# Single scatters, expert weights on ScalarE's queue, and the next stage's loads inside a sort's end: a convolution with a routed expert layer

## The chip, the cores and the metric

The kernel runs on one core of a Trainium2 chip. The core has five engines that run beside each other, each working through its own list of instructions in order: TensorE (PE in the profile, with its weight loads as PEld), VectorE (DVE), ScalarE (ACT), GpSimd (POOL) and SyncE (SP), which here only starts DMA transfers. They meet through semaphores. All transfers run on 16 DMA engines; an instruction of SP, ACT or POOL starts one. The metric is device time of one launch in microseconds (us), lower is better; the time of a kernel is the median of its runs.

## The reference

Each of 8 sequences of 5696 tokens by 128 channels is convolved along the sequence with a filter of the same length (one filter per channel, written in the reference as a product of FFTs). Every token of the result then goes to one of 8 experts, the one with the largest gate logit:

```python
y = irfft(rfft(x, n=2*S) * rfft(h, n=2*S))[:, :S]      # per channel, x is [8, 5696, 128]
logits = y @ w_gate                                     # 45568 tokens, 8 experts
e = argmax(logits); g = softmax(logits)[e]
out = g * (relu(y @ w1[e]) @ w2[e])                     # w1 [8,128,1024], w2 [8,1024,128]
```

## The kernel before

**Stages.** The FFT length is split as 48 x 238, so that the transforms become matmuls with small constant matrices. The 8 sequences are worked in three groups of 2, 3 and 3. Each group passes three phases. Phase A (`steps_a`) transforms along one axis and stores U to DRAM. Phase B (`phase_b`) reads U back in blocks, multiplies by a 96 x 96 matrix for each of 120 frequencies (tile `xp`), by the filter's transform on DVE, adds on POOL (L524), and transforms back (tile `vp`), which ACT copies out for a store to V. Phase C (`phase_c`) reads V, does the last transform (tile `yp`), and finds each token's gate logits, its expert and its rank among the expert's tokens so far. POOL then writes every token's row (128 channels, gate value, token number) to its place in a DRAM table `SR` that is sorted by expert: an indirect DMA of 120 rows (`sort_one`, L608), 128 of them in a group. These are "the sort". When the last ranks of a stretch are known, `tables` works out on DVE which tiles of 256 rows are full and to which expert each belongs; for the very last stretch `fill` also writes dummy rows behind each expert's last token.

Phase A of the next group rides as a guest on phase C's steps (`Guest.begin`, `Guest.end`); what is left is done by `Guest.rest`.

**Experts.** The sorted tokens are taken in four parts of 37, 39, 28 and 81 tiles. Part 0 comes from the first group, parts 1 and 2 from the second, part 3 from the third. `pipeline` is a loop of steps, four to a tile: a tile's rows are loaded from `SR` (`load`, SP), turned on PE, split into two words on ACT and DVE, and each step does a quarter of layer 1 (L1055), the relu on ACT and its rest on DVE (`relu`, L1061, L1063), and a quarter of layer 2 of two steps before (L1075). After four steps ACT copies the result out (`drain`), PE turns it back, DVE multiplies by the gate (`emit`, L1093), and `deliver` scatters the two halves of 128 tokens to the output with two indirect DMAs on POOL (L1119). An expert's weights are four pieces of 512 KB (`load_w`, L1013 to L1028); a register tells whether the tile's expert differs from the one before, and if not the DMA is skipped. Parts 0 to 2 have one set of weight buffers, the last part two.

While a phase C of the second or third group runs, the POOL queue belongs to its sort. Finished expert tiles are then staged in DRAM (`leave`, the `STG` tensor) and brought back later (`recall`, tile `xb`), one in 6 steps; 48 tiles went this way.

**The order of the work.** Nothing is scheduled by the compiler; a small planner writes one fixed order for all engines (`run`). Streams are Python generators, each with a clock of its own that advances by the nanoseconds it yields (an expert step is `STEP = 1420`, an iteration of phase B 0.6 or 0.85 of it, a step of phase C 1.2 or 1.8 of it), and the stream whose clock is furthest behind emits next. After phase B of the first group three streams run: `rest` (phases C and B, group after group), the tail of the weight preparation, and `experts`. So an engine's list is this order filtered by engine, and an instruction that must wait holds everything behind it on its engine. `sort_one(after)` makes a sort scatter wait for a named ACT instruction, to spread the scatters over the stage; each ACT relu, each copy of phase C hands one out. In the first group's phase C the experts are off (`state["alone"]`), as no part is sorted yet. A part may be used once it is sorted, its table is there and (the last one) it is filled (`Part.ready`, `usable`).

Of the kernel before, what the change touches and what calls it, by code (L numbers as in the profile page):

```python
# [54 lines left out]
STAGED = 64  # L55
BACK = 6
HEAD = (0, 8, 8)
LEAD = (0, 6, 6)
# [11 lines left out]
def conv_moe(ctx: ExitStack, tc: tile.TileContext, I, out, B, S, D, E, F, split):  # L70
# [39 lines left out]
    class Part:  # L110
        def __init__(self, s, upto, tiles):
            self.s, self.upto, self.nt = s, upto, tiles
            self.sorted = self.tabled = self.filled = False
            self.lanes, self.fills = [], []

        @property
# [476 lines left out]
    state["base"] = base0  # L593
    state["alone"], state["prepped"], state["defer"] = True, False, False

# [8 lines left out]
    def sort_one(after=None):  # L604
        if not sorts:
            return
        pi, rt, b, pt = sorts.pop(0)
        s = nc.gpsimd.indirect_dma_start(  # L608
            out=SR[:, :],
            out_offset=IndirectOffsetOnAxis(ap=pi[:, b : b + 1], axis=0),  # L610
            in_=rt[:, b, :],
            in_offset=None,
            bounds_check=NROWS - 1,
            oob_is_err=False,
        ).ins
        tc.declare_no_dep(s, group="sr", reason="each row of the sorted tokens is written once, before it is read")
        tc.declare_no_dep(s, group="rows", reason="never a row that a tile has read")
        tc.add_to_no_dep_group("sr", s)
        if len(lanes) >= PIPE_LANES:
            tc.add_manual_dep(s, lanes[-PIPE_LANES].name, SYNC, reason="scatter lane")  # L620
        if after is not None:
            tc.add_manual_dep(s, after.name, SYNC, reason="scatters are spread over the stage")
        lanes.append(s)
        part_row()
        if pt is not None:
            pt.lanes = lanes[-PIPE_LANES:]
            pt.sorted = True

# [8 lines left out]

    def phase_c(gr, guest=None):
        g, nb, cb, cw, NI, ns = gr.g, gr.nb, gr.scb, gr.scw, gr.ni, gr.ns
# [96 lines left out]
        def logit_out(n, k):  # L736
            t = sb.tile([32 * cb, MP], F32, tag="lt", name=f"lt{g}_{n}_{k}", bufs=6)
            done = nc.scalar.copy(t, lbank.pop((n, k))[: 32 * cb, :MP])
            lts[n, k] = t
            sort_one(done.ins)  # L740
            if len(sorts) > ns:
                sort_one()
# [97 lines left out]
        for n in range(n_end + 1):  # L840
            for k in range(nsub):
# [15 lines left out]
                if guest:  # L857
                    guest.begin(1 if k == 0 and n >= sl else 2)
                yield cost if n < nu else cost / 2
# [9 lines left out]
                if k == 0:  # L869
# [6 lines left out]
                    if n - sl - 1 in closes:  # L876
                        pt = closes[n - sl - 1]
                        chores.append(tables(pt, state["base"]))
                        if pt is parts[-1]:
                            chores.append(fill(pt, state["base"]))  # L880
                chore(6)
                if at >= total_sub + LL:
                    break
        while sorts:
            left = len(sorts)
            chore(6)
            yield cost
            if len(sorts) == left:
                sort_one()
# [123 lines left out]
    def load_w(t, n):  # L1013
        pt, j = seq[t]
        z, fixed = home(t), j < sets(t)
        if n == 0:
            ew = nc.sync.value_load(pt.tab[0:1, 1, j : j + 1], min_val=0, max_val=(E - 1) * P)
            ch = None if fixed else nc.sync.value_load(pt.tab[0:1, 2, j : j + 1], min_val=0, max_val=1)
            regs[t] = (ew, ch)
# [5 lines left out]
        kw = {} if fixed else {"cond": ch, "cond_hint": False}  # L1025
        nc.sync.dma_start(dst, WD[n, ds(ew, P), :], **kw)  # L1026
        if n == 3:
# [62 lines left out]

    def emit(t):
        op, xr = obank.pop(t), rows.pop(t)
# [3 lines left out]
        if state["defer"] and slot[0] < STAGED:  # L1096
            leaving.append((STG[slot[0]], xr))
            slot[0] += 1
        else:
            pending.append(xr)  # L1100

    def leave():
        while leaving:
            dst, xr = leaving.pop(0)
            nc.sync.dma_start(dst, xr)
            staged.append(dst)

    def recall(count):
        if coming and coming[0][0] <= count - BACK // 2:
            pending.append(coming.pop(0)[1])  # L1110
        if staged and not coming and not state["defer"] and count % BACK == 0:
# [4 lines left out]
    def deliver():  # L1116
        xr = pending.pop(0)
        for s in range(2):
            sc = nc.gpsimd.indirect_dma_start(  # L1119
                out=out[:, :],  # L1120
                out_offset=IndirectOffsetOnAxis(ap=xr[:, s, D + 1 : D + 2].bitcast(I32), axis=0),
                in_=xr[:, s, :D],
                in_offset=None,
                bounds_check=B * S - 1,
                oob_is_err=False,
            ).ins
            tc.declare_no_dep(sc, group="out", reason="each token is written once")
            tc.add_to_no_dep_group("out", sc)
            if len(outs) >= PIPE_LANES:
                tc.add_manual_dep(sc, outs[-PIPE_LANES].name, SYNC, reason="scatter lane")  # L1130
            outs.append(sc)

    def usable(t):
        return seq[t][0].ready and state["prepped"] and not state["alone"]

    def pipeline(lo, hi):
# [3 lines left out]
        while True:  # L1140
            t, k = step
            while nrow < min(t + 4, hi) and usable(nrow):
                load(nrow)
                seen[nrow] = len(hist)
                nrow += 1
            while nw[0] < min(t + 3, hi) and usable(nw[0]):
                was, n = user[nw[0]], nw[1]
                if was is not None and was >= lo and passed.get((was, n // 2), -1) < 2 * (n % 2) + 1:
                    break
                load_w(nw[0], n)  # L1150
                nw = (nw[0], n + 1) if n < 3 else (nw[0] + 1, 0)
            act = step if t in xts and nw > (t, k // 2) else None
            hist.append(act)
# [5 lines left out]
            if act is None and old is None and to is None and ti is None:  # L1159
                leave()  # L1160
                recall(len(hist))
                if pending:
                    deliver()
                elif t >= hi and not (any(hist[-1 - LAG :]) or staged or coming):
                    return
                yield STEP if turned < nrow or any(hist[-1 - LAG :]) else None
                continue
            leave()
            recall(len(hist))
# [19 lines left out]
            if to is not None:  # L1189
                emit(to)  # L1190
            if pending:
# [9 lines left out]

    def rest():
        for gr in groups:
            if gr.g:
                yield from phase_b(gr)
            guest = Guest(groups[gr.g + 1]) if gr.g + 1 < len(groups) else None
            yield from phase_c(gr, guest)
            if guest:
                yield from guest.rest()

    DONE = object()

    def run(*streams, until=None, stop=()):
        live = [[0.0, i, s, share] for i, (s, share) in enumerate(streams)]
        held = []
        while any(t[2] not in stop for t in live):
            live.sort(key=lambda t: t[:2])
            it = live.pop(0)
            cost = next(it[2], DONE)
            if cost is None:  # L1220
# [107 lines left out]
```

## Time and profile before

| what | us |
|---|---|
| median of 3 runs | 2454.19 |
| lowest and highest of them | 2442.0, 2454.91 |
| the profiled execution, time | 2445.03 |
| the profiled execution, span from first to last instruction | 2443.3 |

The stages in the profiled execution, by the matmul lines that run in them (phase A L295, B L484, C L685, experts L1055):

| stage | from, to (us) |
|---|---|
| phase A of group 0, filter, then phase B of group 0 | 0, 275 |
| phase C of group 0 with phase A of group 1 | 290, 466 |
| end of the first sort, rest of phase A, first expert tiles | 466, 551 |
| phase B of group 1 with experts | 551, 828 |
| phase C of group 1 with phase A of group 2 and experts | 850, 1139 |
| end of the second sort, experts alone | 1139, 1192 |
| phase B of group 2 with experts | 1192, 1534 |
| phase C of group 2 with experts | 1550, 1830 |
| end of the third sort, experts alone | 1830, 1873 |
| experts of the last part, staged tiles brought back until about 2200 | 1873, 2443 |

How to read the profile's rows. A row of the table by stretches gives the stretch, its length, and for each engine its busy time with the count of instructions, then the clock granted to PE as a share of full speed, the share of time that the DMA engines were busy, and GB/s. A row of waits, "engine line <- releaser: total, times, longest", says how long an engine stood before instructions of that line and what ended it. In the order of time a row gives start, duration, engine, line, operation, the tiles written and read, and in brackets the idle time before with what ended it; SPq are the instructions of SP's own list. A row of one line's instructions gives the operation, its count, and shortest, median and longest duration in nanoseconds.

### The profile page before, as it was taken

What the parts mean: (1) busy time and instruction counts of PE and PEld (TensorE: products, weight loads), DVE (VectorE), ACT (ScalarE), POOL (GpSimd) and SP (SyncE); (2) the same over time, 40 slices, a digit from 0 to 9 for tenths busy, and PEclk for the clock granted to TensorE, in tenths of its full rate; (3) what the DMA queues carried; (4) which work ended last, traced back from release to release, by engine and by line L of the source; (5) the groups of instructions that cost most, each with busy time, mean ns of one, the idle gap of its engine ahead of it and who ended that gap; (6) DMA issues with size and microseconds to landing.
All of it is one profiled execution on the core that took longest, in us unless ns stands there. A gap on an engine that the chain in (4) does not pass through costs nothing. (4 is left out here: it accounts for less than half of the span.)

```text
span 2443.3 us, 46852 instructions
## 1 busy us (share of the span) xinstructions
PE 2144.8 (88%) x14070; PEld 1781.7 (73%) x14070; DVE 1582.2 (65%) x3937; ACT 1100.3 (45%) x2389; POOL 1196.8 (49%) x1289
## 2 busy tenths in 40 slices
PE   6899687469999899987899999988987899989997
PEld 4666344257677687777767677877877888889997
DVE  3599554439899677775698798566764444445554
ACT  4677443233333366653333343555643344434443
POOL 4466446715555326665246565166663444443332
PEclk8899899679999999998999999999998999999998
DMA  8999897469999778873788897666653443443330
GB/s 262 304 309 314 256 275 216 116 186 243 241 277 253 195 201 252 248 228 107 197 214 221 251 240 216 172 163 180 169 140 99 142 127 118 130 127 111 111 112 29
DMA packets 246623, 473.55 MB, mean 194 GB/s; under 512 B 34513, under 2 KB 157447, under 8 KB 246368
## 3 DMA queue, kind: packets, MB, share of 16 engines
q1 hardware_dynamic: 222432, 423.43, 61.2%
q0 software_dynamic: 23936, 47.09, 6.4%
q8 instruction: 115, 1.88, 0.3%
q14 instruction: 140, 1.15, 0.2%
HBM read 596.51 MB, written 172.45 MB: 315 GB/s over the span
## 5 line engine op out<-in xcount | busy, mean ns | idle before, releaser
L1063 DVE SCALAR_TENSOR_TENSOR hs<-mh,hs 128x512 fp32r<-128x512 f32 x728 | 501.6, 690 | 509.7 <-ACT hs L1061 402.6
L1055 PE MATMUL mh<-xtb,wb 128*128 128x256 f32 x4368 | 722.9, 301 | 100.7 <-DMA wb<-WD 57.0
L1055 PEld LDWEIGHTS mh<-xtb,wb 128*128 128x128 f32 x4368 | 603.5, 194 | 183.6 <-issue 101.0
L1061 ACT ACTIVATE hs<-mh 128x512 fp32r<-128x512 f32 x728 | 435.0, 598 | 579.7 <-PE mh L1055 452.7
L1075 PE MATMUL ma<-hs,wb 128*128 128x256 f32 x4368 | 669.4, 290 | 13.4 <-DMA wb<-WD 12.0
L1075 PEld LDWEIGHTS ma<-hs,wb 128*128 128x128 f32 x4368 | 586.0, 195 | 17.2 <-DMA wb<-WD 15.2
L608 POOL DMA_INDIRECT SR<-rt,pi x384 | 399.9, 1041 | 367.6 <-ACT hs L1061 113.8
L1119 POOL DMA_INDIRECT out<-xr x268 | 261.3, 975 | 569.6 <-DVE xr L1093 508.5
L524 POOL TENSOR_TENSOR zt<-zt,xs 128x384 f32<-128x384 f32 (+1 forms) x340 | 305.9, 914 | 156.8 <-DVE xs L516 101.9
L540 ACT COPY vt<-vp 96x384 f32<-96x384 f32 (+1 forms) x360 | 158.0, 439 | 376.2 <-PE vp L532 329.1
L532 PE MATMUL vp<-zt,mi 128*96 128x384 f32 (+1 forms) x720 | 273.5, 461 | 8.6 <-POOL zt L524 2.2
L484 PE MATMUL xp<-uq,mt 96*128 96x384 f32 (+1 forms) x720 | 269.9, 457 | 2.1 <-DMA uq<-U 2.1
L509 DVE TENSOR_TENSOR zt<-xp,hh 128x384 f32<-128x384 f32 (+1 forms) x360 | 183.4, 509 | 52.4 <-PE xp L484 33.2
L295 PE MATMUL pa<-xc,fcr 120*120 120x512 f32 x576 | 177.1, 440 | 28.0 <-ACT ut L307 10.5
L532 PEld LDWEIGHTS vp<-zt,mi 128*96 128x96 f32 x720 | 108.1, 163 | 121.1 <-issue 74.7
L516 DVE SCALAR_TENSOR_TENSOR xs<-xp,hh 64x384 f32<-64x384 f32 (+1 forms) x360 | 185.5, 515 | 6.8
L514 DVE TENSOR_TENSOR xs<-xp,hh 64x384 f32<-64x384 f32 (+1 forms) x360 | 182.4, 507 | 6.9
L295 PEld LDWEIGHTS pa<-xc,fcr 120*120 120x120 f32 x576 | 103.7, 197 | 66.5 <-ACT ut L307 10.9
L484 PEld LDWEIGHTS xp<-uq,mt 96*128 96x128 f32 x720 | 117.9, 194 | 23.3 <-issue 10.7
L685 PE MATMUL yp<-vr,gcr 120*120 120x384 f32 x576 | 118.5, 341 | 2.6 <-ACT ut L307 2.5
L673 DVE TENSOR_TENSOR vr<-vq,vr 120x768 fp32r<-120x768 f32 x96 | 92.9, 969 | 33.2 <-ACT vr L672 30.1
L307 DVE COPY ut<-pa 120x512 f32<-120x512 f32 x96 | 65.5, 685 | 73.0 <-PE pa L295 46.4
(123 smaller groups left out, 2228.9 us busy)
## 6 DMA issues: line engine op xcount, KB each, us to landing
wb<-WD SPq DMA_DIRECT2D x728, 512.0 KB
vq<-V SPq DMA_DIRECT2D x64, 720.0 KB
U<-ut SPq DMA_DIRECT2D x48, 720.0 KB
uq<-U SPq DMA_DIRECT2D x60, 576.0 KB
V<-vt SPq DMA_DIRECT2D x60, 576.0 KB
xr<-SR SPq DMA_DIRECT2D x182, 130.0 KB
xt<-x SPq DMA_DIRECT2D x96, 240.0 KB
hh<-HS SPq DMA_DIRECT2D x120, 192.0 KB
```

The lines of the kernel that those rows point to most:

```text
L295: nc.tensor.matmul(banks[m][:QN, :], lhs, rhs, start=(k == 0), stop=(k == len(ops) - 1))
L484: nc.tensor.matmul(xp[:, :cw], mt[:, k0, :], uc, start=True, stop=True)
L509: nc.vector.tensor_tensor(out=zt, in0=x3, in1=hv[:, 0].broadcast_to([P, cb, D]), op=ALU.mult)
L516: nc.vector.scalar_tensor_tensor(out=xs[to], in0=x3[at], scalar=-1.0, in1=him, op0=ALU.mult, op1=ALU.mult)
L524: eng.tensor_tensor(out=zt, in0=zt, in1=xs, op=ALU.add)
L532: nc.tensor.matmul(vp[:K2, :cw], mi[:, k0, :], zt.rearrange("p b d -> p (b d)"), start=True, stop=True)
L608: s = nc.gpsimd.indirect_dma_start(out=SR[:, :], out_offset=IndirectOffsetOnAxis(ap=pi[:, b : b + 1], axis=0), in_=rt[:, b, :], in_offset= ...
L1055: nc.tensor.matmul(hp[:, u, :], wb[:, a, f, :], xt[:, b, :], start=(n == 0), stop=(n == 2))
L1061: done = nc.scalar.activation(hs[:, 0], hp, AF.Relu)
L1063: nc.vector.scalar_tensor_tensor(out=hs[:, 1], in0=hp, scalar=0.0, in1=hs[:, 0].bitcast(F32), op0=ALU.max, op1=ALU.subtract)
L1075: nc.tensor.matmul(accs[t], wb[:, a, f, :], hs[:, b, u, :], start=(k == 0 and u == 0 and n == 0), stop=(k == NPAIR - 1 and u == 1 and n == 2),
L1119: sc = nc.gpsimd.indirect_dma_start(out=out[:, :], out_offset=IndirectOffsetOnAxis(ap=xr[:, s, D + 1 : D + 2].bitcast(I32), axis=0), in_=x ...
```

## The change

1. **One scatter per step.** `pending` holds half tiles, and `deliver` issues one indirect DMA in a step where it issued two. A staged tile leaves three steps after it was emitted (`leave(count)`) instead of at the next step.
2. **Weights on ACT.** `load_w` issues its register loads and DMAs from ACT (`nc.scalar`) for parts 0 to 2; the last part's stay on SP. Weights may be loaded as soon as the part's table is there, ahead of the end of its sort, and in a step they are issued before the rows.
3. **Rows later.** A part's rows are loaded only when the planner's clock stands `SETTLE = 8000` ns past the part's last sort scatter.
4. **Sort handed out faster.** `logit_out` issues a second scatter when more than 2 wait (before: more than `ns` = 6), and steps of phase C that have no synthesis left issue two more.
5. **The sort's end.** `phase_c` now runs the guest's rest and then phase B's part up to its first `yield` (the loads of two blocks) before it hands out the remaining sorts, at a planner cost of `STEP` each. While the experts are off the guest does two of its steps at every step of phase C.

```diff
+SETTLE = 8000
@@ class Part
+            self.since = 0
@@ sort_one
-            pt.sorted = True
+            pt.sorted, pt.since = True, state["now"]
@@ phase_c
-    def phase_c(gr, guest=None):
+    def phase_c(gr, guest=None, after=None):
@@ logit_out
-            if len(sorts) > ns:
+            if len(sorts) > 2:
                 sort_one()
@@ the steps of phase_c
-                    guest.begin(1 if k == 0 and n >= sl else 2)
+                    guest.begin(1 if k == 0 and n >= sl and not state["alone"] else 2)
@@
                 chore(6)
+                if n >= nu:
+                    sort_one()
+                    sort_one()
                 if at >= total_sub + LL:
                     break
+        if guest:
+            yield from guest.rest()
+        if after:
+            yield next(after)
         while sorts:
             left = len(sorts)
             chore(6)
-            yield cost
+            yield STEP
             if len(sorts) == left:
                 sort_one()
@@ load_w
+        eng = nc.sync if pt is parts[-1] else nc.scalar
         if n == 0:
-            ew = nc.sync.value_load(pt.tab[0:1, 1, j : j + 1], min_val=0, max_val=(E - 1) * P)
-            ch = None if fixed else nc.sync.value_load(pt.tab[0:1, 2, j : j + 1], min_val=0, max_val=1)
+            ew = eng.value_load(pt.tab[0:1, 1, j : j + 1], min_val=0, max_val=(E - 1) * P)
+            ch = None if fixed else eng.value_load(pt.tab[0:1, 2, j : j + 1], min_val=0, max_val=1)
...
-        nc.sync.dma_start(dst, WD[n, ds(ew, P), :], **kw)
+        eng.dma_start(dst, WD[n, ds(ew, P), :], **kw)
@@ emit, leave, recall, deliver
-            leaving.append((STG[slot[0]], xr))
+            leaving.append((count, STG[slot[0]], xr))
...
-            pending.append(xr)
+            pending.extend([(xr, 0), (xr, 1)])
...
-    def leave():
-        while leaving:
-            dst, xr = leaving.pop(0)
+    def leave(count):
+        while leaving and leaving[0][0] <= count - 3:
+            _, dst, xr = leaving.pop(0)
             nc.sync.dma_start(dst, xr)
...
-        xr = pending.pop(0)
-        for s in range(2):
-            sc = nc.gpsimd.indirect_dma_start(
...
+        xr, s = pending.pop(0)
+        sc = nc.gpsimd.indirect_dma_start(
...
@@ usable
-        return seq[t][0].ready and state["prepped"] and not state["alone"]
+        pt = seq[t][0]
+        return pt.ready and state["prepped"] and not state["alone"] and state["now"] >= pt.since + SETTLE
@@ pipeline: the weights' loop now stands before the rows' loop
-            while nw[0] < min(t + 3, hi) and usable(nw[0]):
+            while nw[0] < min(t + 3, hi) and seq[nw[0]][0].tabled and state["prepped"]:
@@ rest
+        work = None
         for gr in groups:
-            if gr.g:
-                yield from phase_b(gr)
-            guest = Guest(groups[gr.g + 1]) if gr.g + 1 < len(groups) else None
-            yield from phase_c(gr, guest)
-            if guest:
-                yield from guest.rest()
+            if work:
+                yield from work
+            guest, work = None, None
+            if gr.g + 1 < len(groups):
+                guest, work = Guest(groups[gr.g + 1]), phase_b(groups[gr.g + 1])
+            yield from phase_c(gr, guest, work)
@@ run
+            state["now"] = it[0]
```

More of the change, by code (lines that the diff above doesn't have):

```diff
@@ L593, in conv_moe @@
     state["base"] = base0
-    state["alone"], state["prepped"], state["defer"] = True, False, False
+    state["alone"], state["prepped"], state["defer"], state["now"] = True, False, False, 0
     sorts, row = [], [0]
@@ L1089, in conv_moe, with emit @@
     slot = [0]
-    def emit(t):
+    def emit(t, count):
         op, xr = obank.pop(t), rows.pop(t)
@@ L1109, in recall @@
         if coming and coming[0][0] <= count - BACK // 2:
-            pending.append(coming.pop(0)[1])
+            xr = coming.pop(0)[1]
+            pending.extend([(xr, 0), (xr, 1)])
         if staged and not coming and not state["defer"] and count % BACK == 0:
@@ L1116, in deliver @@
     def deliver():
-        xr = pending.pop(0)
-        for s in range(2):
[L1119 to L1131, printed above, removed]
+        xr, s = pending.pop(0)
+        sc = nc.gpsimd.indirect_dma_start(
+            out=out[:, :],
+            out_offset=IndirectOffsetOnAxis(ap=xr[:, s, D + 1 : D + 2].bitcast(I32), axis=0),
+            in_=xr[:, s, :D],
+            in_offset=None,
+            bounds_check=B * S - 1,
+            oob_is_err=False,
+        ).ins
+        tc.declare_no_dep(sc, group="out", reason="each token is written once")
+        tc.add_to_no_dep_group("out", sc)
+        if len(outs) >= PIPE_LANES:
+            tc.add_manual_dep(sc, outs[-PIPE_LANES].name, SYNC, reason="scatter lane")
+        outs.append(sc)
     def usable(t):
-        return seq[t][0].ready and state["prepped"] and not state["alone"]
+        pt = seq[t][0]
+        return pt.ready and state["prepped"] and not state["alone"] and state["now"] >= pt.since + SETTLE
     def pipeline(lo, hi):
@@ L1141, in pipeline @@
             t, k = step
[L1142 to L1145, printed above, removed]
-            while nw[0] < min(t + 3, hi) and usable(nw[0]):
+            while nw[0] < min(t + 3, hi) and seq[nw[0]][0].tabled and state["prepped"]:
                 was, n = user[nw[0]], nw[1]
@@ L1151, in pipeline @@
                 nw = (nw[0], n + 1) if n < 3 else (nw[0] + 1, 0)
+            while nrow < min(t + 4, hi) and usable(nrow):
+                load(nrow)
+                seen[nrow] = len(hist)
+                nrow += 1
             act = step if t in xts and nw > (t, k // 2) else None
@@ L1159, in pipeline @@
             if act is None and old is None and to is None and ti is None:
-                leave()
+                leave(len(hist))
                 recall(len(hist))
@@ L1163, in pipeline @@
                     deliver()
-                elif t >= hi and not (any(hist[-1 - LAG :]) or staged or coming):
+                elif t >= hi and not (any(hist[-1 - LAG :]) or leaving or staged or coming):
                     return
@@ L1167, in pipeline @@
                 continue
-            leave()
+            leave(len(hist))
             recall(len(hist))
@@ L1189, in pipeline @@
             if to is not None:
-                emit(to)
+                emit(to, len(hist))
             if pending:
```

## The prediction

> **What bounds the kernel now.** I read the engine totals first, then the chain that ended last, then a table of busy time by stretches of the span, and for each stretch with an idle TensorE (PE) the waits and the order of time.
>
> ```profile
> PE 2144.8 (88%) x14070; PEld 1781.7 (73%) x14070; DVE 1582.2 (65%) x3937; ACT 1100.3 (45%) x2389; POOL 1196.8 (49%) x1289
> ```
>
> ```profile
> issue 16%; POOL 6%; POOLq 0%; DMA 0%; SPq 0%
> ```
>
> PE is the busy engine and the others have slack. The chain is of little use here: it follows the output scatters through the last quarter and names "issue", which is no engine. So I take PE's work as fixed and ask where PE stands still. The stretches (length, then busy time of PE, PEld, DVE, ACT, POOL with counts, then granted clock, DMA share, GB/s):
>
> ```profile
> 460.00:490.00 30.00, 5.60 (x14) 3.78 (x14) 13.68 (x68) 3.16 (x6) 24.11 (x29) 0.52 0.36 103
> 490.00:551.00 61.00, 38.70 (x238) 35.23 (x239) 21.01 (x35) 18.92 (x36) 7.12 (x9) 0.76 0.66 187
> 551.00:826.00 275.00, 270.05 (x1428) 196.20 (x1427) 256.02 (x469) 105.26 (x228) 156.01 (x158) 0.99 0.93 247
> 850.00:1120.00 270.00, 249.51 (x1796) 213.60 (x1796) 193.81 (x689) 160.71 (x373) 151.08 (x163) 0.96 0.79 224
> 1120.00:1192.00 72.00, 52.72 (x362) 51.07 (x362) 34.60 (x110) 21.35 (x44) 28.59 (x34) 0.81 0.47 122
> 1545.00:1805.00 260.00, 236.32 (x1896) 211.26 (x1895) 165.78 (x590) 141.62 (x333) 141.67 (x154) 0.99 0.62 165
> 1805.00:1900.00 95.00, 71.64 (x531) 68.14 (x530) 47.94 (x155) 31.15 (x68) 43.91 (x51) 0.89 0.42 122
> ```
>
> Phase B (551 to 826) has PE 98% busy. The three ends of a sort do not: in 460 to 551 PE is idle for 91 - 5.60 - 38.70 = 46.7 us, in 1120 to 1192 for 19.3, in 1805 to 1900 for 23.4, and the granted clock falls to 0.52, 0.81 and 0.89. The fourth soft place is the last part's experts. Layer 1 alone (24 matmuls per tile):
>
> ```profile
> 1900.00:2200.00 300.00, 152.90 (x984) 133.12 (x985) 0.98 0.40 126
> 2200.00:2400.00 200.00, 113.72 (x774) 101.43 (x774) 1.00 0.32 106
> ```
>
> While staged tiles are brought back (until 2200) there are 984/24 = 41.0 tiles in 300 us, 7.32 us each; after that 774/24 = 32.3 in 200 us, 6.20 each. That is 1.12 x 41 = 46 us more than at the later rate.
>
> **The change part by part.** PE's work stays, so a tile that is pushed from one place to another costs nothing by itself; only idle PE time that goes or comes counts.
>
> *End of the first sort.* Waits between 460 and 551, and the first loads and first matmul of the next phase B:
>
> ```profile
> PE mxNone L180 <- DMA xr<-SR: 29.8, 1, 29.8
> PE mh L1055 <- DMA wb<-WD: 15.1, 2, 12.2
> ```
>
> ```profile
> 532.10 0.32 SPq L435 DMA_DIRECT2D uq<-U  x1
> ```
>
> ```profile
> 551.11 0.81 PE L484 MATMUL xp<-uq,mt 96*128 96x384 f32 x2
> ```
>
> Before, an expert's row load sat on SP until the last sort scatter had landed, PE stood 29.8 us, then did the rest of phase A and four tiles, and stood 12.2 us for weights queued on SP behind phase B's twelve first loads (two blocks of mt, uq, two mi, two hh). Now phase A's rest comes before the sort's end (and while the experts are off every step of phase C carries two of its steps; before, each step with a score carried one), the twelve loads are issued at about 466, where PE's 5.60 us of work in the first row end, and the row load waits until 8000 ns of schedule time after the sort, so it blocks nothing. Phase B's first matmul came 19 us after its first load, with expert work in between; 466 + 19 is 485. POOL is busy 24.11 of the 30 us to 490 with sort scatters, and phase B's add (L524) queues behind them, so an earlier issue does not shorten this sort and phase B cannot run before about 486. Some 20 of the 46.7 us stay: **-27** (ends: -5 if the loads land late, -46.7 if all goes).
>
> *Ends of the second and third sort.* There POOL is not the limit; its scatters wait to be handed out:
>
> ```profile
> POOL SR L608 <- ACT hs L1061: 113.8, 42, 44.2
> ```
>
> Each was tied to one expert step. Two more per step once phase C has run out, and a backlog limit of 2 in place of 6, shorten this. In the second, phase B's loads no longer stand in front of weights. In the third, PE waited 9.8 us for weights while SP was held by the fill's loads:
>
> ```profile
> PE mh L1055 <- DMA wb<-WD: 9.8, 3, 5.5
> ```
>
> What stays late there is the table arithmetic on DVE. I take **-10** for each (ends 0 and the idle time, -19.3 and -23.4).
>
> *One scatter per step.* In the bring-back stretch a recalled tile's two scatters follow a fresh tile's two without a gap (first and last of four), and ScalarE (ACT) falls behind:
>
> ```profile
> 2026.50 0.97 POOL L1119 DMA_INDIRECT out<-xr  x1 [3.23 <-DVE xr L1093]
> ...
> 2030.33 0.97 POOL L1119 DMA_INDIRECT out<-xb  x1 [0.30 <-issue]
> ```
>
> ```profile
> 2030.78 0.60 ACT L1061 ACTIVATE hs<-mh 128x512 fp32r<-128x512 f32 x1 [2.37 <-PE mh L1055]
> ```
>
> ```profile
> ACT hs L1061 <- PE mh L1055: 99.9, 123, 1.2
> ```
>
> The last row is 2200 to 2400, with pairs only: no such wait is over 1.2 us. So bursts of four go with the loss, though why ACT starts late the trace does not say. Recalls come once in 6 steps, 1.5 tiles: 27 in the 300 us, 46/27 = 1.7 us each. Spread out, 5 scatters fill 6 steps; the rate is the same and only the gaps differ. Between 0 and -36 I take a third, **-12**. Shorter sort ends also stage fewer tiles: about 6 fewer at 1.7 us, **-10** (0 to -15).
>
> *Weights through ACT.* Parts 0 to 2 have 104 tiles (37, 39, 28). What each issues on SP today, ns as min/median/max, the last row from 551 to 826 alone:
>
> ```profile
> L1017 SPq TENSOR_LOAD <-tab x182: 78/269/1921, 498.8 to 2411.0; - x182
> L1017 SPq FUSED_REGOPS  x182: 152/164/178, 499.2 to 2411.3; - x182
> ```
>
> ```profile
> L1026 SPq FUSED_REGOPS  x728: 2/151/713, 499.4 to 2414.3; - x182
> L1026 SPq MOVE wb<-WD x728: 2/29/704, 499.5 to 2414.5; - x182
> L1026 SPq DMA_DIRECT2D wb<-WD x728: 2/79/658, 499.6 to 2417.0; - x182
> ```
>
> ```profile
> L1017 SPq TENSOR_LOAD <-tab x18: 264/819/1437, 558.5 to 814.0; - x18
> ```
>
> Two register loads of 0.27 + 0.16 us and four DMAs of 0.15 + 0.03 + 0.08 make 1.9 us; with the small gaps I call it 2.5, an estimate, and 3.6 in phase B, where the register load takes 0.82. ACT executes it in order. Queued behind it are the next relu, phase B's copies out of PSUM, phase C's copies and casts; waits that come along (a weight half must have been read by layer 2) are short, since ACT's own copy of layer 2's result waits for nearly the same matmul. In phase B ACT is 38% busy and PE's buffers give it a step. In phase C it is 160.71/270 = 60% and 141.62/260 = 54% busy; 15 tiles (354/24) and 21.5 (516/24) at about 3.2 us bring these to 77% and 81%:
>
> ```profile
> 850.00:1120.00 270.00, 54.19 (x354) 51.22 (x354) 0.96 0.79 224
> 1545.00:1805.00 260.00, 82.86 (x516) 67.57 (x515) 0.99 0.62 165
> ```
>
> What PE waits for ACT today, in the phase C from 1545, then in the one from 850:
>
> ```profile
> PE mx L180 <- ACT ot L1085: 5.7, 5, 2.0
> ...
> PE tp L180 <- ACT rt L700: 2.2, 2, 1.3
> ```
>
> ```profile
> PE pa L295 <- ACT xc L273: 3.0, 1, 3.0
> ...
> PE yp L685 <- ACT ut L307: 2.5, 3, 1.6
> ```
>
> 7.9 and 5.5 us. If such waits grow as busy/(1 - busy), 54 to 81% is 3.6 times and 60 to 77% 2.2 times: +21 and +7. With phase B and the sort ends I take **+30**. The ends: nothing, or all of 104 x 3.2 = 333. The last part's weights stay on SP, so its tiles pay nothing.
>
> *What SP gains.* It no longer waits on PE for weights:
>
> ```profile
> SPq L1026 <- PE ma L1075: 248.1, 134, 8.4
> ```
>
> ```profile
> PE mh L1055 <- DMA wb<-WD: 57.0, 19, 12.2
> ```
>
> Of these 57 us 15.1 and 9.8 are counted above. On a queue of their own, weights need not stand behind SP's larger loads. I take **-5** (ends -20, +10). The Trainium skill, "DMA: Bandwidth & Descriptors", section "Issuing engines are not separate DMA queues", speaks against this: starting DMAs from several engines saves only the time of starting them. By that rule this term is 0 and the sum 5 us higher; the trace of before has a single such queue and cannot show it.
>
> Sum against the profiled execution: 2445.0 - 27 - 10 - 10 - 12 - 10 + 30 - 5 = 2401. That execution stands 9 us under the median shown (2454.19); for the median of the changed kernel I say **2405 us**.
>
> **Rivals.**
> - *ACT hides its share and the bursts were the loss.* ACT costs 5 instead of 30 and spreading gives 30 instead of 12: 2401 - 25 - 18 = 2358. For it: ACT is under 60% busy everywhere. Against: two scatters per tile remain, and the mean rate is unchanged.
> - *Only the first sort's end pays.* The other ends are held by tables on DVE and the bring-back stretch does not move: 2445 - 27 + 30 = 2448, no change. For it: PE waits there for DVE as well as for weights.
> - *ACT becomes the bound: slower.* Without ACT's term the change is worth 74 us, 0.71 us for each of the 104 tiles. If PE waits longer than that for every tile, the kernel is slower; at 1 us a tile it is 2445 - 74 + 104 = 2475. For it: ACT at 80% in phase C, where the next step's transposes need ACT's copy of the step before. The Trainium skill, "Perfetto Trace Analysis", section "DMA Instruction — HWDGE (DVE, Sync)", adds that two issuing sequencers share one generator and wait for its lock; no row here shows such a wait. Against: ACT's waits for PE are long (the 99.9 us above).
>
> **How the numbers follow.** The forecast has 0.48, the rivals 0.24, 0.14 and 0.14. About 0.5% (12 us) is what a measurement of this kernel can tell from no change. Faster 0.72, same 0.14, slower 0.14. The range 2350 to 2465 leaves out the half of the last rival above 2465 and the lower part of the first.
>
> **What would show it.** Right: phase B's first matmul near 486 and no 29.8 us wait; PE idle in the second and third sort's ends down by half; tiles under 7 us while recalls run; ACT's busy time unchanged but PE's waits for ACT in phase C at 25 us and more. Wrong: first-sort idle still over 35 us, or phase C longer than 290 us from ACT waits, or bring-back at 7.3 us a tile with single scatters.

## The result and the profile after

The changed kernel takes 2394.88 us (median of 4 runs, 2378.65 to 2398.87), the kernel before beside it 2453.79 us: a ratio of 0.976, 95% interval 0.9726 to 0.9794. The forecast was 2405 us. The profiled execution has a span of 2397.1 us, 46.2 us less than before. The engine totals of the page after:

```profile
PE 2142.3 (89%) x14070; PEld 1765.9 (74%) x14070; DVE 1583.0 (66%) x3937; ACT 1096.4 (46%) x2389; POOL 1205.5 (50%) x1289
```

PE's work is what it was (2144.8 before); it stands still for 254.8 us where it stood for 298.5. The table by stretches of the changed kernel (columns as in the prediction):

```profile
460.00:507.00 47.00, 18.86 (x44) 9.47 (x42) 27.47 (x92) 3.80 (x9) 31.65 (x36) 0.64 0.87 232
507.00:777.00 270.00, 259.20 (x1313) 178.13 (x1312) 236.78 (x433) 98.48 (x216) 142.22 (x142) 0.99 0.88 233
...
1055.00:1100.00 45.00, 30.33 (x183) 27.84 (x182) 25.02 (x105) 10.82 (x24) 25.87 (x30) 0.75 0.70 181
...
1705.00:1745.00 40.00, 23.04 (x132) 20.81 (x133) 22.66 (x97) 8.00 (x20) 25.87 (x30) 0.67 0.37 105
1745.00:1800.00 55.00, 47.31 (x352) 45.40 (x351) 22.84 (x41) 19.84 (x40) 18.39 (x20) 0.93 0.49 150
```

PE is idle for 28.1 us at the first sort's end (46.7 before), for 14.7 at the second's (19.3), and for 17.0 + 7.7 = 24.7 at the third's (23.4). Only the first is much shorter. In the phase C ahead of it PE now does 12.1 us more work in the same 185 us, where the guest now takes two steps at every step; before, then after:

```profile
275.00:460.00 185.00, 130.10 (x651) 74.98 (x650) 77.11 (x371) 68.97 (x177) 91.82 (x104) 0.88 0.76 219
```

```profile
275.00:460.00 185.00, 142.23 (x710) 83.09 (x711) 89.90 (x396) 77.25 (x196) 100.15 (x113) 0.93 0.84 254
```

The next rows are phase B's first load of U on SP, and PE in order of time, both of the changed kernel:

```profile
477.32 0.32 SPq L437 DMA_DIRECT2D uq<-U  x1
```

```profile
483.02 4.62 PE L486 MATMUL xp<-uq,mt 96*128 96x384 f32 x8 [14.10 <-issue]
495.97 1.62 PE L486 MATMUL xp<-uq,mt 96*128 96x384 f32 x2 [8.33 <-DMA uq<-U]
```

Phase B begins at 483.02, where it began at 551.11; the wait of 29.8 us for the experts' row load is gone, and 14.10 and 8.33 us of waits for phase B's own loads stand in its place (the first row names no releaser; the matmul follows the landing of the load of 477.32).

Experts move from one stretch to another, so stretches are compared at equal tiles. The boundaries are the first and last matmuls of xp and yp in each group (a sort's end runs 20 us into the next phase B); tiles are L1065's matmuls by 24; a tile that moved counts 6.2 us, its time where nothing disturbs it.

| Stretch | before: us (tiles) | after: us (tiles) | change at equal tiles |
|---|---|---|---|
| start to the end of the first phase C | 443.9 (0) | 449.4 (0) | +5 |
| first sort's end | 127.2 (5.2) | 53.7 (0) | -41 |
| second group's phase B, to phase C | 279.5 (19.3) | 289.1 (18.8) | +13 |
| its phase C | 264.1 (14.2) | 256.1 (14.0) | -7 |
| second sort's end | 97.5 (8.9) | 66.5 (4.6) | -4 |
| third group's phase B, to phase C | 338.3 (26.8) | 330.6 (26.9) | -8 |
| its phase C | 257.9 (21.0) | 257.4 (21.2) | -2 |
| third sort's end | 62.0 (4.8) | 43.7 (2.3) | -3 |
| until the last recalled tile is out | 323.9 (44.5) | 296.9 (40.0) | +1 |
| rest | 248.9 (37.2) | 353.7 (54.2) | -1 |

Most of the gain is the first sort's end, 41 of 46 us; the second group's phase B gives 13 us back, the stretches from there to the third sort's end gain 24 together, and the bring-back stretch gives nothing. Layer 1 alone there and in the undisturbed rest, after, and then the bring-back stretch before:

```profile
1746.50:2043.40 296.90, 150.79 (x960) 130.73 (x959) 0.97 0.43 133
2100.00:2300.00 200.00, 113.31 (x773) 101.07 (x772) 1.00 0.39 126
```

```profile
1870.40:2194.40 324.00, 165.31 (x1068) 144.08 (x1068) 0.98 0.40 125
```

960/24 = 40.0 tiles in 296.9 us are 7.42 us each; before it was 324.0/44.5 = 7.28.

The two figures are alike, but what is in them is not. The shorter sorts' ends leave 16.25 tiles of parts 0 to 2 for this stretch, where 3.75 were left before, and these parts have one set of weight buffers. Layer 1 of the changed kernel until the last part begins, then to the end of the stretch:

```profile
1746.50:1874.80 128.30, 63.80 (x390) 54.81 (x390) 0.95 0.43 132
1874.80:2043.40 168.60, 86.99 (x570) 75.92 (x570) 0.99 0.43 133
```

The leftover tiles take 128.3/16.25 = 7.90 us each, the last part's 7.10, where the last part's took 7.30 before (297.5 us for 40.75). PE's waits for weights in the stretch, before and after:

```profile
PE mh L1055 <- DMA wb<-WD: 4.2, 2, 2.7
```

```profile
PE mh L1065 <- DMA wb<-WD: 15.7, 6, 3.6
```

The four waits that this stretch did not have before stand at the 91st, 94th, 97th and 100th tile, all of part 2; the last three stand there in every traced version of the changed kernel, on all chips. So a tile that is pushed to another place is not free here, though the table counts it at 6.2 us.

### The profile page after: what moved, and what is told of

It is laid out like the page before. It is cut to its first block, busy times and chain, and to the rows that moved or that the text cites. A ratio compares the mean times of both kernels' runs of the same rounds, so it can differ in the third digit from the quotient of the medians.

```text
span 2397.1 us, 46980 instructions
## 1 busy us (share of the span) xinstructions
PE 2142.3 (89%) x14070; PEld 1765.9 (74%) x14070; DVE 1583.0 (66%) x3937; ACT 1096.4 (46%) x2389; POOL 1205.5 (50%) x1289
## 5 line engine op out<-in xcount | busy, mean ns | idle before, releaser
L1065 PE MATMUL mh<-xtb,wb 128*128 128x256 f32 x4368 | 717.8, 300 | 64.0 <-DVE hs L1073 23.8
L1065 PEld LDWEIGHTS mh<-xtb,wb 128*128 128x128 f32 x4368 | 600.5, 193 | 142.5 <-issue 51.4
L610 POOL DMA_INDIRECT SR<-rt,pi x384 | 407.7, 1062 | 311.4 <-issue 135.7
L1129 POOL DMA_INDIRECT out<-xr x276 | 270.2, 979 | 554.6 <-DVE xr L1103 500.8
```

The lines of the kernel that those rows point to most:

```text
L610: s = nc.gpsimd.indirect_dma_start(out=SR[:, :], out_offset=IndirectOffsetOnAxis(ap=pi[:, b : b + 1], axis=0), in_=rt[:, b, :], in_offset= ...
L1065: nc.tensor.matmul(hp[:, u, :], wb[:, a, f, :], xt[:, b, :], start=(n == 0), stop=(n == 2))
L1129: sc = nc.gpsimd.indirect_dma_start(out=out[:, :], out_offset=IndirectOffsetOnAxis(ap=xr[:, s, D + 1 : D + 2].bitcast(I32), axis=0), in_=x ...
```

## The experiments

The runs fell on four chips, and the kernel before differs among them by 4%: 2454 us on the first (A), 2359 and 2363 on the next two (B, C), 2449 on the last (D); whether A is one of the others is not known. Ratios go to the kernel before on the same chip.

| Kernel | chip | us | ratio, 95% interval |
|---|---|---|---|
| changed | A | 2394.88 | 0.976, 0.9726 to 0.9794 |
| changed, again | C | 2314.25 | 0.9796, 0.978 to 0.9813 |
| before, again | D | 2453.06 | 1.0005, 0.9974 to 1.0036 |
| both scatters in a step | B | 2308.85 | 0.9778, 0.9749 to 0.9808 |
| all weights on SP | B | 2283.08 | 0.9673, 0.9644 to 0.9702 |
| the same | D | 2377.52 | 0.9723, 0.9693 to 0.9752 |
| before, weights on ACT | B | 2357.76 | 0.9976, 0.9953 to 0.9999 |
| all weights on ACT | B | 2366.11 | 1.0023, 1.0003 to 1.0044 |
| old order at the sorts' ends | C | 2343.55 | 0.9913, 0.9898 to 0.9927 |
| old pace of the sorts | C | 2347.67 | 0.9939, 0.9918 to 0.996 |
| both scatters, weights on SP | C | 2291.99 | 0.970, 0.9684 to 0.9716 |
| weights partly on ACT | D | 2386.04 | 0.9758, 0.9731 to 0.9784 |
| more loads on ACT | D | 2572.77 | 1.0524, 1.0494 to 1.0554 |

### Both scatters of a tile in one step

```diff
-            if pending:
+            for _ in range(min(2, len(pending))):
                 deliver()
```

> The changed kernel, but both scatters of a tile are issued in one step again. Theory A (the single scatters made a new wait: in the changed kernel's last part the load of a new tile's rows stands on SP for 77.5 us, in 12 waits between 1745 and 2042, until an old tile's late scatters have freed its row buffer, and the last part's weights queue behind it): these waits on SP fall under 10 us, PE's waits for weights in the bring-back stretch fall from 15.7 us to under 5, a tile there takes no more than before the change, and the time is 8 to 15 us under the changed kernel, near 2383. Theory B (the prediction's: bursts of four scatters cost the stretch its 1.1 us a tile, and single ones save 12 to 36 us): 12 us or more over the changed kernel, 2407 and up.

0.9778 beside 0.9796 for the changed kernel on another chip: no difference that the intervals show. Theory A fell at its root. SP's waits in the row load, first in the changed kernel (1745 to 2042), then in this one (whole span):

```profile
SPq L1015 <- DMA out<-xr: 77.5, 12, 8.3
```

```profile
SPq L1015 <- DMA out<-xr: 82.7, 15, 8.0
```

They do not come from single scatters. Nor is anything urgent behind them: in the changed kernel all of them fall before 1900, and until 1870 ACT still issues the weights, so SP's queue has time to spare. A long wait on a queue is a loss only if something that is needed stands behind it. Theory B fell here too, but chip B cannot test its premise, as is shown below.

### Where the weights are loaded

The changed kernel with all weights on SP, twice; then the other way round.

```diff
-        eng = nc.sync if pt is parts[-1] else nc.scalar
+        eng = nc.sync
```

> The changed kernel, but all weights are loaded through SP's queue again. Theory A (ACT's 104 loads cost the path next to nothing, since PE's waits for ACT in the phases C are 11.6 and about 6 us where 7.9 and 5.5 were before, and a queue of their own lets weights pass SP's waiting stores): 5 to 20 us over the changed kernel, 2400 to 2415, with more of PE's waits for weights. Theory B (the prediction's terms of +30 and -5): 25 us under the changed kernel, 2370.

> The changed kernel with all weights on SP once more, beside the next kernel on one chip: all theories expect 0.967, as measured first.

On chip B this is 0.9673 where the changed kernel on chip C has 0.9796: ACT's loads cost 1.2%, 29 us (0.0123 of 2361), give or take 8 by the two intervals together. That is the size of the prediction's +30 and -5, and theory A fell there. On chips D and A it is 0.9723 beside 0.976, 9 us, which the intervals do not tell from nothing. Both pairs of chips agree on one place. The second group's phase B, first with weights on ACT (changed kernel, chip C), then on SP (chip B):

```profile
482.00:746.40 264.40, 254.43 (x1272) 173.64 (x1271) 235.60 (x432) 95.46 (x208) 139.69 (x141) 0.99 0.90 238
```

```profile
482.90:730.00 247.10, 243.05 (x1269) 174.85 (x1268) 233.85 (x430) 95.55 (x207) 139.02 (x140) 1.00 0.96 255
```

The same 16.0 tiles and the same blocks take 17.3 us longer, 1.1 us a tile; between chips A and D it is 264.9 against 249.0. What ACT waited for in this stretch on chip C, and PE's weight loads with it:

```profile
ACT vt L542 <- DMA wb<-WD: 22.0, 14, 3.2
```

```profile
PEld xp L486 <- ACT vt L542: 10.3, 9, 1.3
```

ACT's copies of phase B out of PSUM stand behind its weight issue for 22.0 us, and PE waits for the copies; with weights on SP ACT has no such row. In the third group's phase C ACT costs 12.5 us (242.1 against 229.6, 21.2 tiles), and in the third group's phase B it saves 9 at equal tiles (300.0 for 23.7 tiles against 307.5 for 23.5).

```diff
-        eng = nc.sync if pt is parts[-1] else nc.scalar
+        eng = nc.scalar
```

> The changed kernel with the last part's weights on ACT's queue too, so that no weight stands behind a row load that waits on SP. Theory A (SP's held row loads are what delays the last part's weights): PE's waits for weights between 1745 and 2042 fall from 15.7 us to under 4, and the time is 5 to 12 us under the changed kernel, near 2386. Rival (78 more tiles at about 2 us of ACT's sequencer delay the activations where a tile takes 6.2 us of PE and PE never rests): 10 us or more over it, 2405 and up, with waits of PE for ACT after 2042, where there are none now.

The rival was right: 1.0023, 2.3% over the changed kernel. Layer 1 late in the last part, here and in the changed kernel on chip C, and PE's wait here from 1971 on:

```profile
2000.00:2300.00 300.00, 165.86 (x1052) 139.94 (x1050) 1.00 0.31 97
```

```profile
2000.00:2250.00 250.00, 142.72 (x973) 127.47 (x972) 1.00 0.34 110
```

```profile
PE mh L1065 <- ACT hs L1071: 10.0, 22, 0.9
```

Its weight loads wait as well:

```profile
PEld mh L1065 <- ACT hs L1071: 23.7, 53, 1.1
```

1052/24 = 43.8 tiles at 6.84 us against 40.5 at 6.17: 0.67 us a tile. PE has nothing else to do there while a relu is late, and ACT is 43% busy (it was 49%): a busy share says nothing of an engine that must answer within a step.

```diff
 # the kernel before
+        eng = nc.sync if pt is parts[-1] else nc.scalar
...
-        nc.sync.dma_start(dst, WD[n, ds(ew, P), :], **kw)
+        eng.dma_start(dst, WD[n, ds(ew, P), :], **kw)
```

> The kernel before with one edit: the weights of all parts but the last go through ACT's queue. Theory A (ACT hides them and SP is relieved): 0 to 15 us under the kernel before, 2439 to 2454; the first tiles after the first sort no longer wait 12.2 us for weights behind the next phase's first loads. Theory B (the prediction's sum of +30 and -5): 2479.

0.9976: 6 us under the kernel before, at the edge of its interval, as theory A had it. So the same edit is worth a little in the old order and costs 29 us in the new one, on chips B and C. In the old order it still leaves the largest single wait, in this run:

```profile
PE mxNone L180 <- DMA xr<-SR: 34.5, 1, 34.5
```

Moving weights off SP does not clear the first sort's end; the row load still holds it. A reading that fits both: what ACT relieves SP of at the sorts' ends the new order relieves it of as well, and ACT's cost is left. It was not tried by itself.

### More loads on ACT

```diff
             regs[t] = (ew, ch)
+            if eng is nc.scalar:
+                for _ in range(4):
+                    eng.value_load(pt.tab[0:1, 1, j : j + 1], ...)
```

> The changed kernel, where ACT makes four more register loads for each of the 104 tiles whose weights it issues, which are not used: at 0.28 to 0.41 us for the load and 0.16 for the operation behind it about 2 us more on ACT's sequencer for each tile, near a doubling of its 2.4. Theory A (what the weights cost on ACT is the time in which its sequencer issues them, some 29 us of the path for about 250 us of issue): 20 to 30 us over the changed kernel, ratio 0.988 to 0.993. Rival (the cost lies in waits, for buffers that PE still reads and for completion semaphores that both queues use in turn, and the issue itself hides): within 8 us of it, 0.978 to 0.983.

Theory A by its sign, but far above its size: 1.0524 against 0.976, 187 us, 1.8 for each of 104 tiles. The added instructions, ns as min/median/max:

```profile
L1032 ACTq TENSOR_LOAD <-tab x416: 5/277/1649, 466.0 to 2030.8; - x139
L1032 ACTq FUSED_REGOPS  x416: 15/147/699, 466.4 to 2031.1; - x139
```

Four times 0.277 + 0.147 us at the median, with the longer ones, are some 2 us a tile. The third group's phase C and PE's longest wait in it, here and then in the changed kernel on chip A:

```profile
1520.10:1819.30 299.20, 246.70 (x1886) 218.77 (x1886) 162.57 (x607) 141.03 (x334) 144.57 (x160) 0.95 0.51 132
```

```profile
PE tp L182 <- ACT rt L702: 34.7, 17, 3.1
```

```profile
1445.40:1702.80 257.40, 235.78 (x1886) 210.11 (x1887) 162.68 (x587) 141.44 (x332) 146.79 (x159) 0.99 0.59 155
```

```profile
PE tp L182 <- ACT rt L702: 5.8, 11, 1.1
```

41.8 us more for 21.2 tiles: 2.0 us a tile, all that was added. The first 2.5 us of issue (261 us on ACT's three lines of `load_w` in the changed kernel, for 104 tiles) nearly hide on ACT over the whole kernel, the next 2 are paid in full in this stretch.

### The changed kernel again, and the old order at the sorts' ends

> The changed kernel once more, on the same chip as the three beside it and, it is hoped, as the runs so far: all theories expect a ratio to the kernel before of about 0.976, as first measured. It is the base that the others are compared with.

It gives 0.9796 on chip C, within the first interval's reach (0.9726 to 0.9794 and 0.978 to 0.9813 overlap). Beside it:

```diff
-            yield from phase_c(gr, guest, work)
+            yield from phase_c(gr, guest)
+            if guest:
+                yield from guest.rest()
```

(with phase B run whole behind it, as before)

> The changed kernel, but the next group's phase B is begun only when the sort has ended, and the guest's rest comes behind it, as before. Prediction's theory (the ends of the sorts are worth 27 us at the first and some of 10 at the others): 25 to 40 us over the changed kernel, with PE idle for 15 us or more longer at the first sort's end. Rival (with weights on ACT the loads of phase B no longer stand in front of them, and the wait of 8000 ns keeps the row load back, so that the old order costs little): within 8 us of it.

29 us over the changed kernel on the same chip (2343.55 and 2314.25): the size the prediction's theory named, but not its place. The first sort's end takes 50.5 us, 51.3 in the changed kernel, though PE is idle in it for 33.3 us against 26.7. Half of the old wait for the row load is back, between phase B's first matmuls; the changed kernel has no such row:

```profile
PE mxNone L182 <- DMA xr<-SR: 15.2, 1, 15.2
```

Part of that loss falls behind the cut, 20 us into phase B. The loss stands at equal tiles in the second group's phase B and the way to its phase C (+19), the second sort's end (+12) and the way to the last phase C (+10).

### Old pace of the sorts

```diff
-            if len(sorts) > 2:
+            if len(sorts) > ns:
                 sort_one()
...
-                if n >= nu:
-                    sort_one()
-                    sort_one()
```

> The changed kernel, but the sort's scatters are handed out as before: a backlog of six before a second one goes with a step, and no two more per step once phase C has run out. Prediction's theory (this brings most of 10 us at each of the second and third sort's ends): 8 to 20 us over the changed kernel. Rival (what is late there is the table arithmetic behind the scatters): within 5 us.

33 us over the changed kernel (2347.67 and 2314.25), above the range, and again elsewhere: at equal tiles +19 up to the end of the first phase C, +11 on the way to the last phase C, +9 at the third sort's end, +4 at the second's and in the second group's phase B, -14 in the bring-back. What POOL waited for in the first sort: with the old pace, in the changed kernel beside it, then on chip A in the kernel before and in the changed kernel:

```profile
POOL SR L610 <- ACT rt L702: 28.9, 18, 4.1
```

```profile
POOL SR L610 <- ACT rt L702: 3.6, 3, 1.8
```

```profile
POOL SR L608 <- ACT rt L700: 30.2, 14, 5.1
```

```profile
POOL SR L610 <- ACT rt L702: 22.7, 12, 5.9
```

On chip C the first sort was bound less by POOL than by how its scatters were handed out; its 96 scatters (the two later sorts have 144 each) span 160.2 us with the old pace and 138.9 with the new. On chip A the same sort went from 160.7 to 151.2 us only, and most of the wait stayed; why is open.

### Scatters in pairs with weights on SP, and weights on ACT for 27 tiles

> The changed kernel with both scatters of a tile in one step and all weights on SP's queue: of the change only the order at the sorts' ends and their pace are left. In the runs so far weights on SP gave a ratio to the kernel before of 0.9673 and pairs 0.9778. Theory A (single scatters pay where SP also carries the weights, since a burst costs a step there): 0.970 to 0.976. Rival (single scatters gain nothing anywhere and only make row loads wait): 0.967 or under.

0.970 beside 0.9673 with single scatters: in the direction of theory A, but on another chip and with overlapping intervals. By the medians single scatters are worth 6 us here, by the ends of the two intervals anything from -4 to 17.

```diff
-        eng = nc.sync if pt is parts[-1] else nc.scalar
+        eng = nc.scalar if pt is parts[1] and j < 27 else nc.sync
```

> The changed kernel with weights on SP, but for the first 27 tiles of the second part, which run beside the last phase B: these stay on ACT. In the runs so far this phase B took 300 us with ACT's queue and 307 and 314 with SP's, while the first phase B took 264 against 247 and the last phase C 242 against 230. Theory A (ACT's queue helps where SP's loads of phase B stand in front of many weights, and costs elsewhere): 5 to 10 us under the kernel beside it with all weights on SP, ratio 0.963 to 0.965. Rival (the gain in that phase B is only a shift between stretches): within 4 us of it, 0.966 to 0.968.

Theory A fell: 0.9758 beside 0.9723 on one chip. The third group's phase B is 3 us shorter (300.8 and 303.9), and the whole is not faster. Of all versions, the changed kernel with its weights on SP has the lowest ratios, 0.9673 and 0.9723; the one with pairs, 0.970, is not told apart from it.

### The kernel before, on another chip

> The kernel before, for a trace on the chips of the experiments, whose times for it are some 2360 where the first were 2454. All theories expect a ratio of 1.00. If the loss of 1.1 us a tile in the bring-back stretch belongs to the kernel, a tile there takes about 7.0 here; if it belonged to the first chip's run, 6.4, as in the run with only the weights moved to ACT.

Its bring-back stretch takes 324.1 us for 44.5 tiles, 7.28 us each, as on chip A. On chip B the kernel before with weights on ACT, whose last part is the same, takes 282.7 us for 44.3 tiles: 6.38. So most of the loss there goes with the chip. The changed kernel loses on chips B and C too: a tile of the stretch takes 6.8 to 7.1 us in four of its versions (as it is, with pairs, with weights on SP, with both), and PE waits 17 to 22 us for weights there, where the kernel before with weights on ACT has 3.8. The bring-back stretch of the changed kernel with weights on SP, layer 1 alone, on chip D and on chip B:

```profile
1716.90:2021.70 304.80, 151.40 (x960) 133.55 (x960) 0.95 0.41 130
```

```profile
1655.30:1926.50 271.20, 143.90 (x954) 127.94 (x954) 0.97 0.45 145
```

7.62 and 6.82 us a tile, by the same program. On chip D in order of time, POOL, then ACT, then PE:

```profile
1830.27 0.97 POOL L1129 DMA_INDIRECT out<-xr  x1 [3.17 <-DVE xr L1103]
1831.54 0.97 POOL L1129 DMA_INDIRECT out<-xr  x1 [0.30 <-issue]
1832.82 0.97 POOL L1129 DMA_INDIRECT out<-xb  x1 [0.30 <-issue]
1834.10 0.97 POOL L1129 DMA_INDIRECT out<-xb  x1 [0.31 <-issue]
```

```profile
1835.94 0.60 ACT L1071 ACTIVATE hs<-mh 128x512 fp32r<-128x512 f32 x1 [2.50 <-PE mh L1065]
```

```profile
1832.56 0.88 PE L1065 MATMUL mh<-xtb,wb 128*128 128x256 f32 x6
```

PE has ended this relu's matmuls at 1833.44; ACT starts it at 1835.94, after the fourth scatter. Counted over the span, a relu starts over 0.5 us after its matmuls and ACT's instruction before it have ended 26 times on chip D, each time with three or four scatters begun in the 6 us before, and never with two or fewer; on chip B the same kernel has 150 relus behind four scatters, and none is late. In the kernel before on chip A 30 late relus fall in the bring-back and add up to 48.8 us, close to the 46 us that the prediction found there; in the changed kernel on chip A it is 20 and 27.8 us. No run on chip A or D takes the bursts away, so that they are the cause is not shown.

## Why the prediction was right

The time fell within the range and 10 us under the forecast, but the sum holds errors that cancel (its own figures, 2401 and the 9 us, give 2410), and that it came so close is in part luck.

**End of the first sort, -27.** Right in mechanism, undersized: -41 at equal tiles on chip A, and -43 between before and the version with weights on SP on chip D (128.5 us with 5.3 tiles to 52.4 with none). In the prediction's own measure, PE's idle time, 18.6 us went there (28.1 us stayed, 20 predicted) and 12.1 in the phase C ahead of it, which the prediction put at nothing. The first matmul of phase B came at 483.02 (486 predicted), by two errors that cancel: the first load of U started at 477.32 and not at 466, as it had to wait for the stores of U, and the matmul came 5.7 us behind it and not 19. POOL's scatters were not the limit: the last ended at 489.1, and PE then waited until 495.97 for the next load of U. Which edit did it is open in part: ACT's queue alone does not take the wait for the row load away, the old pace does not bring it back, and the old order brings back 15.2 us of it; the later row load (with the weights' loop ahead of the rows') and the guest's two steps are left, and neither was undone by itself. One step was wrong: "an earlier issue does not shorten this sort". It was read from the last 30 us, where POOL is full; over the whole sort POOL waited 30.2 us, and the new pace takes 21 us off the sort on chip C; on chip A the whole change takes 9.5 us off it.

**Ends of the second and third sort, -10 each.** Oversized: -4 and -3 at equal tiles. On chip C the pace does help there (4 and 9 us), and on the way to the next phase, but on chip A little is left of it.

**One scatter per step, -12, and fewer staged tiles, -10.** This failed: +1 at equal tiles. 44 tiles are staged, 4 fewer and not 6, and a tile takes 7.42 us. Two changes cancel in the +1. The tiles left over from part 2 cost 24 us more than before over their 6.2 us (27.6 for 16.25 tiles against 3.2 for 3.75), 11.7 of it in the four waits for weights: the prediction put that at nothing when it called a pushed tile free. The last part's tiles cost 23 us less, mostly because 17 fewer of them fall into the stretch; each takes 7.10 us for 7.30. The step that failed is "Spread out, 5 scatters fill 6 steps". Issued one per step, the scatters still queue on POOL behind the first one, which waits for DVE's scaling, and then go without a gap: 23 runs of four in the bring-back where there were 26. Late relus do go with bursts of four, on chips A and D, and not on B and C.

**Weights through ACT, +30.** Right in sum on chips B and C (29 us net, with the -5 for SP in it), 9 us and unresolved on A and D. But the term was worked out on the kernel before, and there the same edit saves 6 us (0.9976), so the sum was met partly by luck. The place was half wrong: 17 us fall into the second group's phase B, which the prediction passed over because PE's buffers give ACT a step there, and 12.5 into the last phase C (+21 predicted). The third rival's turning point was 0.71 us a tile; 29/104 = 0.28 was paid, and 2 us more of issue were enough to pass it.

**What SP gains, -5.** Small, as said: -9 in the third group's phase B on chips B and C, -3 on D. PE's waits for weights fell from 69.0 us in the whole kernel before to 26.2 in the changed one (chip A), but also from 70.9 to 32.3 with all weights on SP (chip D): most of that comes from the other edits, not from the queue. The Trainium skill, "DMA: Bandwidth & Descriptors", section "Issuing engines are not separate DMA queues", expects no more than the saved issue time, and the traces agree: with two queues the second group's phase B moved 238 GB/s, with one 255, for the same blocks and tiles. The lock between two issuing sequencers of "Perfetto Trace Analysis", section "DMA Instruction — HWDGE (DVE, Sync)" (the Trainium skill), does not show in these rows: SP's loads of mi on chip A before and after, ns as min/median/max, became no longer.

```profile
L438 SPq DMA_DIRECT2D mi<-miq x180: 310/470/2408, 105.1 to 1501.7; - x180
```

```profile
L440 SPq DMA_DIRECT2D mi<-miq x180: 311/436/1993, 106.8 to 1401.8; - x180
```

## What to carry to other kernels

Spreading instructions over the steps of a program spreads them in time only if their engine keeps step with the program: on an engine that waits for one input and has the rest queued behind it, they come out in a burst again. Issuing conditional loads from a compute engine's queue is cheap until it is not: here 2.5 us a tile cost 0.28 and the next 2 us cost 1.8, so undo that part alone before keeping it. Work that is moved meets other limits in its new place: tiles of part 2 that had run beside a phase C stood for their weights when they ran alone. And ask whether a sort, a scatter or a load is bound by its engine over the whole stage, not in its last microseconds.

## What the runs showed of the hardware

Two things were not expected. After three or four scatters in a row ACT starts relus late on chips A and D (by 0.5 to 2.8 us on D) and not on B and C; in the version with weights on SP, 92 of the 98 us by which chip D is slower than B fall into the first, second and third phase C, the second sort's end and the bring-back, where scatters run (+11, +20, +20, +8, +34), and the two phases B and the rest differ by under 4 each. What differs in the chips stays open.

And two queues of loads are not independent in this program. In the trace all loads of SP and ACT count their completion in turn on the same eight counters, and each waits until the last load on its counter has completed. SP's waits in the second group's phase B of the changed kernel on chip C, and then a load of ACT and one of SP on the same counter:

```profile
SPq L440 <- DMA wb<-WD: 45.1, 12, 10.1
```

```profile
545.82 1.89 ACTq L1036 DMA_DIRECT2D wb<-WD  x2
```

```profile
545.95 5.45 SPq L440 DMA_DIRECT2D mi<-miq  x2
```

ACT's load at 545.82 is skipped by its condition and counts at once, and SP's load of mi, on the same counter, follows at 545.95; ACT's next, at 547.35, is taken, and SP's next load, on that one's counter, follows at 551.07, when it has landed. ACT's loads themselves wait for PE to have read the buffer. PE was not held by it here (0.3 us for uq in this stretch); what it costs elsewhere was not tried.
